# Routing steps of a fused attention and expert kernel held in PSUM

## The chip, the cores and the metric

The kernel runs on one core of a Trainium2 chip. The core has five engines with a queue each: PE (TensorE) multiplies matrices and transposes, DVE (VectorE) and ACT (ScalarE) do element-wise work and reductions, POOL (GpSimd) adds and subtracts in SBUF here and issues indirect DMAs, SP (SyncE) issues the other DMAs. [...] The metric is the device time of one execution in microseconds (us); before the change three runs took 1650.76, 1652.64 and 1657.65 us.

## The reference

Three layers follow each other. The first is attention with keys and values pooled by 8, over 8 batches, 8 heads, 576 rows of 64 values (4608 tokens of 512). The second sends each token to the one of 8 experts with the largest logit. The third is a gated layer with 1536 hidden values.

```python
k_p = k.reshape(B, H, Sp, pool, D).mean(axis=3)
v_p = v.reshape(B, H, Sp, pool, D).mean(axis=3)
scores = scale * np.matmul(q, k_p.transpose(0, 1, 3, 2))
attn = softmax(scores)                      # max subtracted
x = np.matmul(attn, v_p)                    # 4608 tokens x 512

logits = x @ w_gate
expert_idx = np.argmax(logits, axis=1)
for e in range(E):
    mask = expert_idx == e
    h = np.maximum(x[mask] @ w1[e], 0.0)
    out[mask] = gate_w[mask, None] * (h @ w2[e])

xn = x / rms * rms_g
g = xn @ w_gate2
out = (g * sigmoid(g) * (xn @ w_val)) @ w_out
```

## The kernel before

**The attention loop.** `for n in range(NTL)` (L809) goes over 36 tiles of 128 tokens. A tile's body is written out in a fixed order: transposes of its probabilities (emit_pt, L417), the exponentials of the tile after it (emit_exp), the turned queries three tiles ahead (emit_qt), place a, the scores two tiles ahead (emit_sc, PSUM tile sc), place b, the product with the values (emit_av, PSUM tile av; DVE then divides, L450 to L462, and writes the logits of the tile into lgs), the store of the tile before, and the places c, d and e. Each engine runs its own instructions in the order in which they were written.

**The places.** Everything else is put into the places a to e of a tile by `plan(n, where, f)`: loads and sums of keys and values (POOL adds groups of rows, L269 to L295, DVE some of them, L291), their transposes and scalings (rows_v, prep_vg, prep_k, place_v), the routing, the choice of the first expert, and the loads and splits of its weights. The table ORDER says at which place the steps on keys and values stand.

**Shared PSUM.** The pool `ps` has two buffers of one bank each, with the tags "pp" and "pq". A new tile of a tag waits until everybody has read the one before. "pq" holds turned queries; "pp" holds the turned sums of keys and values (ptk, ptv, pk), the values times the gate (pvg), half of the placed values (pv), ranks (rk), counts (cn0, cn) and half of a slot's turned rows (px).

**Routing.** Groups of four or five tiles are routed together (route_steps, L481). r1 finds each token's expert on DVE: the maximum of the logits (rmx), an equality (roh), a number for each candidate (rcd), its minimum (rcm), and the one-hot row rob. It stands in place d of the tile behind the group: tiles 4, 9, 13, 18, 22, 27, 31, 34, and inside the last tile. r3, two tiles later in place d, ranks the tokens: PE counts into rk, and nine DVE steps follow (L512 to L530), which mask, add, turn the rank into an address by bit operations, and bring the running counts run_c forward. r4 scatters the token numbers with indirect DMAs from POOL's queue.

**The first slot.** From tile 21 on the kernel chooses the expert with the most tokens (choose to choose_5), gathers its first 256 rows (first_rows, L655; tile xg), copies their logits to lg0 with POOL (L661), and turns the rows (xpose, L580) in tiles 32 and 33. The weights of this expert are loaded from tile 25 on (load_w) and split into a rounded part and a rest (split_w, L170): ACT casts (L148), POOL subtracts (L149), in 16 halves of 128x512. The first product with them stands in tile 34.

**Behind the loop** come 26 slots of 256 tokens for the experts and then the third layer; both are PE's matmuls almost throughout and are not touched.

Of the kernel before, what the change touches and what calls it, by code (L numbers as in the profile page):

```python
# [9 lines left out]
F32 = mybir.dt.float32  # L10
F32R = mybir.dt.float32r
BF16 = mybir.dt.bfloat16
I32 = mybir.dt.int32
U32 = mybir.dt.uint32
AF = mybir.ActivationFunctionType
ALU = mybir.AluOpType
AX = mybir.AxisListType
# [5 lines left out]
DM = 512  # L23
E = 8
F1 = 1024
F2 = 1536
T = 256
# [6 lines left out]
XW = DM + E  # L34
CUT = 18
# [16 lines left out]

R3 = [13, 17]

CW = [19, 30, 36, 46, 35, 52]

PLAIN = (0, 1, 2, 3, 4, 5)

# [24 lines left out]
def fused(ctx: ExitStack, tc: tile.TileContext, q, k, v, moe_w_gate, moe_w1, moe_w2,  # L83
          w_gate, w_val, w_out, rms_g, cst, out):
    nc = tc.nc
# [37 lines left out]
    lg0 = const.tile([128, 2, E], F32, name="lg0")  # L123
# [6 lines left out]
    def apart(i, key):  # L130

        i = getattr(i, "ins", i)
        nc.gpsimd.memset(spare, 0.0)
        for o in groups_.setdefault(key, []):
            tc.declare_no_dep(i, o, reason="rows of their own")
        groups_[key].append(i)
# [7 lines left out]
    def wtile(dt, name):  # L144
        return wp.tile([128, 1024], dt, tag="w", name=name)

    def split(hi, lo, src, eng=nc.vector):
        nc.scalar.copy(out=hi, in_=src)  # L148
        eng.tensor_tensor(out=lo, in0=src, in1=hi, op=ALU.subtract)  # L149
# [21 lines left out]
    def split_w(i, half, fresh=False):  # L171
        if fresh:
            for w, nm in ((w1h, "w1h"), (w1l, "w1l")) if i < 4 else ((w2h, "w2h"), (w2l, "w2l")):
                w[i % 4] = wtile(F32R, f"{nm}{i % 4}")
        hi, lo = (w1h[i], w1l[i]) if i < 4 else (w2h[i - 4], w2l[i - 4])
        c = slice(512 * half, 512 * half + 512)
        split(hi[:, c], lo[:, c], st[i][:, c], nc.gpsimd)
# [3 lines left out]
    sm_p = rctx.enter_context(tc.tile_pool(name="sm", bufs=2))  # L181
    sm1 = rctx.enter_context(tc.tile_pool(name="sm1", bufs=1))
    ps = rctx.enter_context(tc.tile_pool(name="ps_a", bufs=1, space=PSUM))
# [297 lines left out]
    def route_steps(n0, n1):  # L481
        n = n1 - n0
        t = {}

        def r1():
            lg = lgs[:, n0:n1]
            mx = sm_p.tile([128, n, 1], F32, tag="rmx", name="rmx")
            nc.vector.tensor_reduce(out=mx, in_=lg, axis=AX.X, op=ALU.max)
            mb = mx.to_broadcast([128, n, E])
            oh = sm1.tile([128, n, E], F32, tag="roh", name="roh")  # L490
            nc.vector.tensor_tensor(out=oh, in0=lg, in1=mb, op=ALU.is_equal)
            ie = cc[:, C_IE:C_IE + E].unsqueeze(1).to_broadcast([128, n, E])
            cand = sm1.tile([128, n, E], F32, tag="rcd", name="rcd")
            nc.vector.scalar_tensor_tensor(out=cand, in0=oh, scalar=-16.0, in1=ie, op0=ALU.mult, op1=ALU.add)
            cm = sm1.tile([128, n, 1], F32, tag="rcm", name="rcm")
            nc.vector.tensor_reduce(out=cm, in_=cand, axis=AX.X, op=ALU.min)
            ob = sm_p.tile([128, n, E], BF16, tag="rob", name="rob")
            nc.vector.tensor_tensor(out=ob, in0=cand, in1=cm.to_broadcast([128, n, E]), op=ALU.is_equal)
            t["ob"] = ob

        def r3():

            ob = t["ob"]
            rk = ps.tile([128, n, E], F32, tag="pp", name="rk")
            nc.tensor.matmul(rk, lhsT=tri, rhs=ob, start=True, stop=False)
            nc.tensor.matmul(rk, lhsT=ones, rhs=off_c.unsqueeze(1).to_broadcast([128, n, E]), start=False, stop=False)
            for j in range(n - 1):
                nc.tensor.matmul(rk[:, j + 1:], lhsT=ones, rhs=ob[:, j:j + 1].to_broadcast([128, n - 1 - j, E]),
                                 start=False, stop=False)
            nc.tensor.matmul(rk, lhsT=ones, rhs=run_c.unsqueeze(1).to_broadcast([128, n, E]), start=False, stop=True)  # L510
            pos = sm_p.tile([128, n, E], F32, tag="rpo", name="rpo")
            nc.vector.tensor_tensor(out=pos, in0=rk, in1=ob, op=ALU.mult)  # L512
            pf = sm_p.tile([128, n], F32, tag="rpf", name="rpf")
            nc.vector.tensor_reduce(out=pf, in_=pos, axis=AX.X, op=ALU.add)
            pi = sm_p.tile([128, n], I32, tag="rpi", bufs=4, name="rpi")
            nc.vector.tensor_copy(out=pi, in_=pf)
            q_ = pf.bitcast(I32)
            nc.vector.tensor_scalar(out=q_, in0=pi, scalar1=15, scalar2=4,
                                    op0=ALU.bitwise_and, op1=ALU.logical_shift_left)
            nc.vector.scalar_tensor_tensor(out=q_, in0=pi, scalar=-T, in1=q_,  # L520
                                           op0=ALU.bitwise_and, op1=ALU.bitwise_or)
            nc.vector.tensor_scalar(out=pi, in0=pi, scalar1=4, scalar2=15,
                                    op0=ALU.logical_shift_right, op1=ALU.bitwise_and)
            nc.vector.tensor_tensor(out=pi, in0=q_, in1=pi, op=ALU.bitwise_or)
            if n == 1:
                nc.vector.tensor_tensor(out=run_c, in0=run_c, in1=ob[:, 0], op=ALU.add)
            else:
                more = sm_p.tile([128, E], F32, tag="rmo", name="rmo")
                nc.vector.tensor_reduce(out=more, in_=ob.rearrange("p n e -> p e n"), axis=AX.X, op=ALU.add)
                nc.vector.tensor_tensor(out=run_c, in0=run_c, in1=more, op=ALU.add)  # L530
            t["pi"] = pi
            if n1 == CUT:
                nc.vector.tensor_copy(out=run_1, in_=run_c)

        def r4(j):
            def f():
                i = nc.gpsimd.indirect_dma_start(
                    out=ord_d[:, :], out_offset=bass.IndirectOffsetOnAxis(ap=t["pi"][:, j:j + 1], axis=0),
                    in_=tok[:, n0 + j:n0 + j + 1], in_offset=None)
                apart(i, "ord")  # L540
            return f

        return r1, r3, [r4(j) for j in range(n)]

    xts, hs, p1 = {}, {}, []
# [34 lines left out]
    def xpose(s, c):  # L580

        px_ = px(c)
        for d in range(2):
            for z in range(2):
                nc.tensor.transpose(px_[:, d, 128 * z:128 * z + 128],
                                    xg[s][:, z, (2 * c + d) * 128:(2 * c + d) * 128 + 128], ident)
        hi, lo = (x[:, 2 * c:2 * c + 2] for x in xts[s])
        nc.scalar.copy(out=hi, in_=px_)
        nc.vector.tensor_tensor(out=lo, in0=px_, in1=hi, op=ALU.subtract)
        if c and s:  # L590
            gate_of(s)


    ev, xg, first = {}, {}, {}
# [60 lines left out]
    def first_rows():  # L655
        xg[0] = x_p.tile([128, 2, XW], F32, tag="xg0", bufs=1, name="xg0")
        for z in range(2):
            nc.gpsimd.indirect_dma_start(
                out=xg[0][:, z], out_offset=None, in_=x_d[0:CUT * 128, :],
                in_offset=bass.IndirectOffsetOnAxis(ap=tok0[:, z:z + 1], axis=0))  # L660
        nc.gpsimd.tensor_copy(out=lg0, in_=xg[0][:, :, DM:XW])  # L661
        xts[0] = tuple(wtile(F32R, "xt0").rearrange("p (c t) -> p c t", c=4) for _ in range(2))

    def second_tokens():
# [10 lines left out]
    def px(c):  # L675
        return ps.tile([128, 2, T], F32, tag=("pq", "pp")[c], name="px")
# [4 lines left out]
    def plan(n, where, f):  # L681
        at.setdefault((n, where), []).append(f)
# [13 lines left out]
    for name, soon, later in ORDER:  # L696
        for m in range(1, 4):
            i = soon if m == 1 else later
# [10 lines left out]
    for n0, n1 in groups:  # L709
# [9 lines left out]
        for j, f in enumerate(r4):  # L719
            plan(n1 + R3[1] // 5 + j // 2, "abcde"[R3[1] % 5], f)  # L720
    for i, f in zip(CW, (choose, first_expert, first_tokens, first_rows)):
        plan(CUT + i // 5, "abcde"[i % 5], f)
    for i in range(8):
        plan(CUT + 7 + i // 2, "ac"[i % 2], lambda i=i: load_w(i, ev[0], True))
        plan(CUT + 9 + (i + 1) // 2, "ca"[i % 2], lambda i=i: split_w(i, 0, True))
        plan(CUT + 9 + (i + 1) // 2, "eb"[i % 2], lambda i=i: split_w(i, 1))
    plan(CUT + 4, "e", choose_2)
    plan(CUT + 7, "e", choose_3)
    plan(CUT + 8, "e", choose_4)
    plan(CUT + 9, "e", choose_5)  # L730
    plan(SECOND - 2, "a", second_tokens)
    plan(SECOND, "c", second_rows)
    plan(NTL - 4, "b", lambda: xpose(0, 1))
    plan(NTL - 3, "a", lambda: xpose(0, 0))
    plan(NTL - 3, "b", start_slots)

# [445 lines left out]
    for s in range(SURE):  # L1182
# [15 lines left out]
        a = unit_steps(s, 0)  # L1198
# [206 lines left out]
```

## Time and profile before

| what | value |
|---|---|
| three runs | 1650.76, 1652.64, 1657.65 us |
| the profiled execution's own time | 1641.33 us |
| its span in the profile | 1639.5 us |
| PE busy | 1590.8 us, 97% of the span |
| DVE busy | 850.8 us, 52% |
| ACT busy | 500.8 us, 31% |
| POOL busy | 263.5 us, 16% |
| attention loop | about the first 228 us |

The profile shows one execution. Its span is the time from the first to the last instruction that the hardware profiler recorded; the execution's own time is 1.83 us longer. "Busy" is the time in which an engine worked on an instruction; the rest is idle. A row of the timeline gives the start, the length, the engine, the line of the kernel, the operation, what it writes and reads, and how many instructions were merged; in brackets stand the idle time of the engine before it and what ended that.

### The profile page before, as it was taken

The page shows a single profiled execution, that of the slowest core. Times are in us where ns is not written, and L with a number is a line of the kernel's source. Part 1 is how long each engine was busy: PE and PEld are TensorE (multiplying, and loading weights), DVE is VectorE, ACT ScalarE, POOL GpSimd, SP SyncE. Part 2 cuts the span into 40 slices and gives each one's busy share as a digit, 9 for nine tenths or more (in the row PEclk, how much of TensorE's full clock was granted, in tenths as well). Part 3 has the DMA queues.
Part 4 walks back from the last instruction along what each step waited for, and adds up shares of the span by engine and source line. Part 5 has one row for each costly group of instructions (what it writes and reads, how often), then busy time and mean ns, then how long its engine had stood idle before and what let it go on. Part 6 is the DMA issues. An engine that isn't in the chain of part 4 may idle for free. (4 is left out here: it accounts for less than half of the span.)

```text
span 1639.5 us, 26570 instructions
## 1 busy us (share of the span) xinstructions
PE 1590.8 (97%) x9331; PEld 1373.4 (84%) x9332; DVE 850.8 (52%) x1824; ACT 500.8 (31%) x1052; POOL 263.5 (16%) x362
## 2 busy tenths in 40 slices
PE   9999899999999989999999999999999999999997
PEld 6888889977888888889788888888888888888886
DVE  7688876788758687225433433334343333443222
ACT  3454633545434453222212122121211212122121
POOL 5776552110111101103000000000000000000000
PEclk9999999999999999999999999999999999999999
DMA  7965636476746464219201000010010001000000
GB/s 216 287 190 152 178 94 214 139 264 229 245 147 216 156 219 123 67 35 322 59 13 33 20 14 26 14 39 13 20 33 14 26 13 39 14 1 26 1 26 14
DMA packets 125373, 161.97 MB, mean 99 GB/s; under 512 B 38544, under 2 KB 83728, under 8 KB 125216
## 3 DMA queue, kind: packets, MB, share of 16 engines
q1 hardware_dynamic: 113440, 124.13, 25.5%
q0 software_dynamic: 11776, 35.91, 7.0%
q8 instruction: 78, 1.28, 0.3%
q14 instruction: 79, 0.65, 0.1%
HBM read 116.92 MB, written 43.08 MB: 98 GB/s over the span
## 5 line engine op out<-in xcount | busy, mean ns | idle before, releaser
L1302 DVE SCALAR_TENSOR_TENSOR th<-th,g 128x512 f32<-128x512 f32 (+1 forms) x120 | 76.1, 634 | 469.0 <-ACT th L1301 469.0
L1299 PE MATMUL g<-xh,rl 128*128 128x512 f32 (+1 forms) x576 | 217.3, 377 | 0.0
L1298 PE MATMUL g<-xl,rh 128*128 128x512 f32 (+1 forms) x576 | 217.3, 377 | 0.0
L1297 PE MATMUL g<-xh,rh 128*128 128x512 f32 (+1 forms) x576 | 217.2, 377 | 0.0
L1301 ACT ACTIVATE th<-g 128x512 f32<-128x512 f32 (+1 forms) x120 | 66.8, 557 | 461.9 <-PE g L1299 461.9
L1328 POOL DMA_INDIRECT out_dram<-o,tk x36 | 34.6, 962 | 815.7 <-ACT o L1327 786.4
L1323 PE MATMUL po<-rl,a 128*128 128x512 f32 x360 | 140.3, 390 | 1.5 <-DMA rl<-scr 1.5
L1322 PE MATMUL po<-rh,a 128*128 128x512 f32 x360 | 140.2, 389 | 0.0
L1324 PE MATMUL po<-rh,a 128*128 128x512 f32 x360 | 140.1, 389 | 0.0
L1298 PEld LDWEIGHTS g<-xl,rh 128*128 128x128 f32 x576 | 108.3, 188 | 20.3
L1297 PEld LDWEIGHTS g<-xh,rh 128*128 128x128 f32 x576 | 108.3, 188 | 20.3
L1299 PEld LDWEIGHTS g<-xh,rl 128*128 128x128 f32 x576 | 108.4, 188 | 20.0
L148 ACT CAST a<-th 128x512 fp32r<-128x512 f32 (+1 forms) x120 | 69.3, 578 | 167.2 <-DVE th L1303 167.2
L554 PE MATMUL p<-xh,w1h 128*128 128x256 f32 x672 | 109.3, 285 | 10.8 <-DVE hl L557 8.3
L149 DVE TENSOR_TENSOR a<-th,a 128x512 fp32r<-128x512 f32 (+1 forms) x120 | 76.7, 639 | 77.3 <-ACT a L148 77.3
L1297 PE MATMUL g<-xh,uh 128*128 128x512 f32 (+1 forms) x288 | 108.7, 378 | 1.7 <-DVE th L1303 1.7
L1298 PE MATMUL g<-xl,uh 128*128 128x512 f32 (+1 forms) x288 | 108.6, 377 | 0.0
L1299 PE MATMUL g<-xh,ul 128*128 128x512 f32 (+1 forms) x288 | 108.6, 377 | 0.0
L554 PE MATMUL p<-xh,w1l 128*128 128x256 f32 x672 | 107.3, 282 | 0.0
L554 PE MATMUL p<-xl,w1h 128*128 128x256 f32 x672 | 106.8, 281 | 0.0
L554 PEld LDWEIGHTS p<-xh,w1h 128*128 128x128 f32 x672 | 93.2, 191 | 15.9 <-DVE hl L557 9.4
L557 DVE SCALAR_TENSOR_TENSOR hl<-p,hh 128x256 fp32r<-128x256 f32 x168 | 70.6, 421 | 62.0 <-ACT hh L556 54.4
(289 smaller groups left out, 3019.2 us busy)
## 6 DMA issues: line engine op xcount, KB each, us to landing
st<-in_moe_w_dram SPq DMA_DIRECT2D x64, 512.0 KB
y_d<-ys SPq DMA_DIRECT2D x39, 257.0 KB
v<-in_v_dram SPq DMA_DIRECT2D x32, 288.0 KB
y<-y_d SPq DMA_DIRECT2D x68, 128.0 KB
x_d<-x SPq DMA_DIRECT2D x32, 260.0 KB
q<-in_q_dram SPq DMA_DIRECT2D x15, 512.0 KB
scr<-uh SPq DMA_DIRECT2D x13, 512.0 KB
scr<-ul SPq DMA_DIRECT2D x13, 512.0 KB
```

The costliest lines, as they stand in the source:

```text
L148: nc.scalar.copy(out=hi, in_=src)
L149: eng.tensor_tensor(out=lo, in0=src, in1=hi, op=ALU.subtract)
L554: nc.tensor.matmul(a, lhsT=w[d][:, fs], rhs=x[:, d], start=j + d == 0, stop=j == 2 and d == 3)
L557: nc.vector.scalar_tensor_tensor(out=lo, in0=a, scalar=0.0, in1=hi, op0=ALU.max, op1=ALU.subtract)
L1297: nc.tensor.matmul(g[:, j], lhsT=wh[:, sl], rhs=hi[:, d], start=d == 0, stop=False)
L1298: nc.tensor.matmul(g[:, j], lhsT=wh[:, sl], rhs=lo[:, d], start=False, stop=False)
L1299: nc.tensor.matmul(g[:, j], lhsT=wl[:, sl], rhs=hi[:, d], start=False, stop=d == 3)
L1301: nc.scalar.activation(out=th, in_=g[:, 0], func=AF.Tanh, scale=0.5)
L1302: nc.vector.scalar_tensor_tensor(out=th, in0=th, scalar=1.0, in1=g[:, 0], op0=ALU.add, op1=ALU.mult)
L1322: nc.tensor.matmul(po, lhsT=a[:, 0, tsl], rhs=wh[:, sl], start=c == 0, stop=False)
L1323: nc.tensor.matmul(po, lhsT=a[:, 0, tsl], rhs=wl[:, sl], start=False, stop=False)
L1324: nc.tensor.matmul(po, lhsT=a[:, 1, tsl], rhs=wh[:, sl], start=False, stop=c == NC2 - 1)
```

## The change

r1 allocates a PSUM tile rw of tag "pp", copies the logits into it, and holds the equality and the candidates there. r3 holds the sum, the address and the counts' increment in the unused part of rk's bank. The logits lg0 are copied by ACT in xpose, directly behind the transposes, where POOL copied them behind the gather. The splits of the weights get their places from a table SPLIT, both halves of one in the same place. choose_2 goes from place e of tile 22 to d of tile 23, choose_5 from e of tile 27 to a of tile 28. The shortened list CW drops a number that nothing read.

```diff
-CW = [19, 30, 36, 46, 35, 52]
+CW = [19, 30, 36, 46, 35]
+
+SPLIT = [(27, "a"), (27, "c"), (28, "a"), (28, "c"), (30, "c"), (31, "a"), (32, "a"), (32, "c")]
...
-            oh = sm1.tile([128, n, E], F32, tag="roh", name="roh")
-            nc.vector.tensor_tensor(out=oh, in0=lg, in1=mb, op=ALU.is_equal)
+            w = ps.tile([128, 3, n, E], F32, tag="pp", name="rw")
+            nc.vector.tensor_copy(out=w[:, 0], in_=lg)
+            nc.vector.tensor_tensor(out=w[:, 1], in0=w[:, 0], in1=mb, op=ALU.is_equal)
...
-            cand = sm1.tile([128, n, E], F32, tag="rcd", name="rcd")
-            nc.vector.scalar_tensor_tensor(out=cand, in0=oh, scalar=-16.0, in1=ie, op0=ALU.mult, op1=ALU.add)
+            nc.vector.scalar_tensor_tensor(out=w[:, 2], in0=w[:, 1], scalar=-16.0, in1=ie, op0=ALU.mult, op1=ALU.add)
...
-            nc.vector.tensor_tensor(out=ob, in0=cand, in1=cm.to_broadcast([128, n, E]), op=ALU.is_equal)
+            nc.vector.tensor_tensor(out=ob, in0=w[:, 2], in1=cm.to_broadcast([128, n, E]), op=ALU.is_equal)
...
-            rk = ps.tile([128, n, E], F32, tag="pp", name="rk")
+            rt = ps.tile([128, 64], F32, tag="pp", name="rk")
+            rk = rt[:, 0:n * E].rearrange("p (n e) -> p n e", e=E)
...
-            pf = sm_p.tile([128, n], F32, tag="rpf", name="rpf")
+            pf = rt[:, 48:48 + n]
             nc.vector.tensor_reduce(out=pf, in_=pos, axis=AX.X, op=ALU.add)
+            pw = rt[:, 56:56 + n].bitcast(I32)
+            nc.vector.tensor_copy(out=pw, in_=pf)
+            q_ = sm_p.tile([128, n], I32, tag="rpf", name="rpf")
+            nc.vector.tensor_scalar(out=q_, in0=pw, scalar1=15, scalar2=4,
+                                    op0=ALU.bitwise_and, op1=ALU.logical_shift_left)
...
-                more = sm_p.tile([128, E], F32, tag="rmo", name="rmo")
+                more = rt[:, 40:40 + E]
...
+        if c and not s:
+            nc.scalar.copy(out=lg0, in_=xg[0][:, :, DM:XW])
...
-        nc.gpsimd.tensor_copy(out=lg0, in_=xg[0][:, :, DM:XW])
...
-        plan(CUT + 9 + (i + 1) // 2, "ca"[i % 2], lambda i=i: split_w(i, 0, True))
-        plan(CUT + 9 + (i + 1) // 2, "eb"[i % 2], lambda i=i: split_w(i, 1))
-    plan(CUT + 4, "e", choose_2)
+        n, w = SPLIT[i]
+        plan(n, w, lambda i=i: split_w(i, 0, True))
+        plan(n, w, lambda i=i: split_w(i, 1))
+    plan(CUT + 5, "d", choose_2)
...
-    plan(CUT + 9, "e", choose_5)
+    plan(CUT + 10, "a", choose_5)
```

Where it tells in the order of the instructions. On PE, tile 27 before: the product with the values (av), then in place e the values times the gate (pvg), then the next tile's transposes (pt). In brackets stands on which engines' signals a row waits.

```order
L443 MATMUL av<-vbd_131,ptsb 128x146 [waits Activation_49]
L443 MATMUL av<-vbd_131,ptsb 128x146 x2
L349 MATMUL pvg<-wg,vt 72x16 [waits Activation_49]
L349 MATMUL pvg<-wg,vt 72x16 x3
L425 MATMUL pt<-cc,pe 96x128 x6
```

The same place on PE in the changed kernel:

```order
L445 MATMUL av<-vbd_131,ptsb 128x146 [waits Activation_49]
L445 MATMUL av<-vbd_131,ptsb 128x146 x2
L351 MATMUL pvg<-wg,vt 72x16 [waits DVE_49,Activation_49]
L351 MATMUL pvg<-wg,vt 72x16 x3
L427 MATMUL pt<-cc,pe 96x128 x6
```

The rows stand where they stood; the first pvg now waits for DVE as well, for its instruction that writes rob in the same tile. On DVE the same tile before: the end of the division (x), r1, choose_5 (quant), second_tokens (tokc), the maximum of the next scores (mx).

```order
L462 TENSOR_TENSOR x<-av,rs 128x512 [waits DMAHW6_49]
L488 TENSOR_REDUCE rmx<-lgs 128x5
L491 TENSOR_TENSOR roh<-lgs,rmx 128x40 [waits DVE_49]
L494 SCALAR_TENSOR_TENSOR rcd<-roh,cc 128x40 [waits DVE_49]
L496 TENSOR_REDUCE rcm<-rcd 128x5 [waits DVE_49]
L498 TENSOR_TENSOR rob<-rcd,rcm 128x40 [waits DVE_49]
L638 TENSOR_SCALAR m_2499<-cc 128x8
L639 SCALAR_TENSOR_TENSOR quant<-m_2499 128x8 [waits DVE_49]
L640 TENSOR_SCALAR quant<-lam 128x8
L641 MEMSET quant 128x8
L665 TENSOR_SCALAR tokc<-tok_88 128x2 [waits DMASW5_49,DMASW4_49]
L408 TENSOR_REDUCE mx<-sc 128x8 [waits PE_49]
```

And on DVE in the changed kernel:

```order
L464 TENSOR_TENSOR x<-av,rs 128x512 [waits DMAHW6_49]
L490 TENSOR_REDUCE rmx<-lgs 128x5
L493 COPY rw<-lgs 128x40 [waits Activation_49]
L494 TENSOR_TENSOR rw<-rw,rmx 128x40 [waits DVE_49]
L496 SCALAR_TENSOR_TENSOR rw<-rw,cc 128x40 [waits DVE_49]
L498 TENSOR_REDUCE rcm<-rw 128x5 [waits DVE_49]
L500 TENSOR_TENSOR rob<-rw,rcm 128x40 [waits DVE_49]
L644 TENSOR_SCALAR m_2530<-cc 128x8
L645 SCALAR_TENSOR_TENSOR quant<-m_2530 128x8 [waits DVE_49]
L646 TENSOR_SCALAR quant<-lam 128x8
L647 MEMSET quant 128x8
L670 TENSOR_SCALAR tokc<-tok_88 128x2 [waits DMASW5_49,DMASW4_49]
```

The copy has come in, and waits until ACT has read what was in the buffer; choose_5 keeps its neighbours. On POOL, from the gather (xg) of tile 27 on, before: the copy of the logits (lg) stands behind the gather, and all subtractions (w1l) behind the copy.

```order
L658 DMA xg_2451<-x_d,tok_88 128x520 [waits DMAHW4_49,DMAHW3_49,DMAHW2_49]
L658 DMA xg_2451<-x_d,tok_88 128x520
L661 COPY lg_91<-xg_2451 128x16 [waits DMASW3_49,DMASW2_49]
L149 TENSOR_TENSOR w1l_2476<-st_2285,w1h_2475 128x512 [waits DMAHW1_49,Activation_49]
L149 TENSOR_TENSOR w1l_2476<-st_2285,w1h_2475 128x512 [waits Activation_49]
L149 TENSOR_TENSOR w1l_2528<-st_2330,w1h_2527 128x512 [waits DMAHW4_49,Activation_49]
```

The same stretch of POOL in the changed kernel:

```order
L151 TENSOR_TENSOR w1l_2425<-st_2280,w1h_2424 128x512 [waits DMAHW1_49,Activation_49]
L151 TENSOR_TENSOR w1l_2425<-st_2280,w1h_2424 128x512 [waits Activation_49]
L664 DMA xg_2452<-x_d,tok_88 128x520 [waits DMAHW4_49,DMAHW3_49,DMAHW2_49]
L664 DMA xg_2452<-x_d,tok_88 128x520
L151 TENSOR_TENSOR w1l_2476<-st_2325,w1h_2475 128x512 [waits DMAHW4_49,Activation_49]
```

The first two subtractions now stand ahead of the gather, the copy is gone, and nothing on POOL waits for the gather's landing.

## Rows read from the trace of the kernel before

**Rows 1.** The page, part 1: busy us, share of the span, instructions.

```profile
PE 1590.8 (97%) x9331; PEld 1373.4 (84%) x9332; DVE 850.8 (52%) x1824; ACT 500.8 (31%) x1052; POOL 263.5 (16%) x362
```

**Rows 2.** Stretches: us; PE, PEld, DVE, ACT, POOL busy; PE clock, DMA, GB/s.

```profile
160.00:170.00 10.00, 9.53 (x83) 8.85 (x83) 7.71 (x26) 3.28 (x8) 5.56 (x7) 0.83 0.52 164
200.00:210.00 10.00, 8.63 (x52) 8.62 (x52) 7.09 (x21) 4.88 (x11) 9.15 (x11) 0.68 0.09 28
340.00:350.00 10.00, 7.92 (x54) 7.72 (x53) 9.01 (x18) 5.83 (x12) 0.54 (x1) 0.83 0.87 294
390.00:400.00 10.00, 8.33 (x63) 7.68 (x63) 9.12 (x14) 8.14 (x15) 0.84 (x2) 1.00 0.89 324
```

**Rows 3.** Waits of PE, 0 to 260 us: total us, times, longest.

```profile
PE sc L401 <- DVE rs L450: 4.7, 1, 4.7
PE sc L404 <- DVE rs L450: 2.9, 2, 2.1
...
PE pv L361 <- ACT qt L391: 0.7, 1, 0.7
PE av L443 <- DVE x L462: 0.5, 2, 0.3
```

**Rows 4.** Timeline, tiles 30 to 32: start, us, engine, instruction, idle before.

```profile
189.79 9.87 POOL L149 TENSOR_TENSOR w1l<-st,w1h 128x512 fp32r<-128x512 f32 x8
...
192.41 1.15 DVE L516 CAST rpi<-rpf 128x5 int32<-128x5 f32 x1
...
198.63 1.05 DVE L530 TENSOR_TENSOR run_c<-run_c,rmo 128x8 bf16<-128x8 bf16 x1
...
201.37 2.26 PE L401 MATMUL sc<-kbd,qt 128*128 128x144 f32 x8 [4.73 <-DVE rs L450]
```

**Rows 5.** Timeline, tile 22, a step of r1.

```profile
155.04 1.49 DVE L498 TENSOR_TENSOR rob<-rcd,rcm 128x32 bf16<-128x32 f32 x1
```

**Rows 6.** Timeline, tile 27: PE's pvg and DVE's r1.

```profile
179.51 0.64 PE L349 MATMUL pvg<-wg,vt 128*72 128x16 f32 x8
...
181.19 0.18 DVE L488 TENSOR_REDUCE rmx<-lgs 128x5 f32<-128x40 f32 x1
181.41 0.20 DVE L491 TENSOR_TENSOR roh<-lgs,rmx 128x40 f32<-128x40 f32 x1
...
182.11 0.20 DVE L498 TENSOR_TENSOR rob<-rcd,rcm 128x40 bf16<-128x40 f32 x1
```

**Rows 7.** Timeline, tiles 4 and 13: r1's start and PE's place e.

```profile
48.74 0.18 DVE L488 TENSOR_REDUCE rmx<-lgs 128x4 f32<-128x32 f32 x1
48.94 1.59 PE L327 MATMUL pk<-cc,se 96*128 96x48 f32 x8 [0.83 <-ACT kbd L331]
...
103.34 1.65 PE L361 MATMUL pv<-vau,both 72*96 72x146 f32 x12
...
105.05 0.17 DVE L488 TENSOR_REDUCE rmx<-lgs 128x4 f32<-128x32 f32 x1
```

**Rows 8.** Timeline, tile 7: r3's first step, POOL, and pvg.

```profile
65.01 0.45 POOL L295 TENSOR_TENSOR sv<-v 72x128 f32<-72x128 f32 x1 [3.41 <-ACT vau L315]
65.18 0.18 DVE L512 TENSOR_TENSOR rpo<-rk,rob 128x32 f32<-128x32 f32 x1
...
66.35 0.69 PE L349 MATMUL pvg<-wg,vt 128*72 128x16 f32 x8
```

**Rows 9.** Timeline, tiles 32 and 35: r1 and PE's next use of pp.

```profile
208.05 0.18 DVE L488 TENSOR_REDUCE rmx<-lgs 128x4 f32<-128x32 f32 x1
...
208.44 0.60 PE L585 MATMUL px<-cc,xg 128*128 128x128 f32 x4
...
223.65 0.19 PE L505 MATMUL rk<-rob,tri 128*128 128x32 bf16 x1
...
224.03 0.17 DVE L498 TENSOR_TENSOR rob<-rcd,rcm 128x8 bf16<-128x8 f32 x1
```

**Rows 10.** Timeline: POOL's copy of the first slot's logits.

```profile
189.63 0.19 POOL L661 COPY lg<-xg 128x16 f32<-128x16 f32 x1 [11.63 <-DMA xg<-x_d,tok]
```

More of the change, by code (lines that the diff above doesn't have):

```diff
@@ L489, in r1 @@
             mb = mx.to_broadcast([128, n, E])
-            oh = sm1.tile([128, n, E], F32, tag="roh", name="roh")
-            nc.vector.tensor_tensor(out=oh, in0=lg, in1=mb, op=ALU.is_equal)
+            w = ps.tile([128, 3, n, E], F32, tag="pp", name="rw")
+            nc.vector.tensor_copy(out=w[:, 0], in_=lg)
+            nc.vector.tensor_tensor(out=w[:, 1], in0=w[:, 0], in1=mb, op=ALU.is_equal)
             ie = cc[:, C_IE:C_IE + E].unsqueeze(1).to_broadcast([128, n, E])
-            cand = sm1.tile([128, n, E], F32, tag="rcd", name="rcd")
-            nc.vector.scalar_tensor_tensor(out=cand, in0=oh, scalar=-16.0, in1=ie, op0=ALU.mult, op1=ALU.add)
+            nc.vector.scalar_tensor_tensor(out=w[:, 2], in0=w[:, 1], scalar=-16.0, in1=ie, op0=ALU.mult, op1=ALU.add)
             cm = sm1.tile([128, n, 1], F32, tag="rcm", name="rcm")
-            nc.vector.tensor_reduce(out=cm, in_=cand, axis=AX.X, op=ALU.min)
+            nc.vector.tensor_reduce(out=cm, in_=w[:, 2], axis=AX.X, op=ALU.min)
             ob = sm_p.tile([128, n, E], BF16, tag="rob", name="rob")
-            nc.vector.tensor_tensor(out=ob, in0=cand, in1=cm.to_broadcast([128, n, E]), op=ALU.is_equal)
+            nc.vector.tensor_tensor(out=ob, in0=w[:, 2], in1=cm.to_broadcast([128, n, E]), op=ALU.is_equal)
             t["ob"] = ob
@@ L512, in r3 @@
             nc.vector.tensor_tensor(out=pos, in0=rk, in1=ob, op=ALU.mult)
-            pf = sm_p.tile([128, n], F32, tag="rpf", name="rpf")
+            pf = rt[:, 48:48 + n]
             nc.vector.tensor_reduce(out=pf, in_=pos, axis=AX.X, op=ALU.add)
-            pi = sm_p.tile([128, n], I32, tag="rpi", bufs=4, name="rpi")
[L516 to L524, printed above, removed]
+            pw = rt[:, 56:56 + n].bitcast(I32)
[3 more added lines that the diff above has]
+                                    op0=ALU.bitwise_and, op1=ALU.logical_shift_left)
+            nc.vector.scalar_tensor_tensor(out=q_, in0=pw, scalar=-T, in1=q_,
+                                           op0=ALU.bitwise_and, op1=ALU.bitwise_or)
+            nc.vector.tensor_scalar(out=pw, in0=pw, scalar1=4, scalar2=15,
+                                    op0=ALU.logical_shift_right, op1=ALU.bitwise_and)
+            pi = sm_p.tile([128, n], I32, tag="rpi", bufs=4, name="rpi")
+            nc.vector.tensor_tensor(out=pi, in0=pw, in1=q_, op=ALU.bitwise_or)
             if n == 1:
```

## The prediction

> **What bounds the kernel now.** I read the page first: PE is busy for 97% of the span, DVE for half of it [rows 1]. The change touches only the first 230 us, the attention loop of 36 tiles, so the question is what PE does there. PE's waits over the first 260 us come next: the reader is to see how little there is to win, and that the largest items are PE waiting for DVE [rows 3]. Scores wait for their PSUM tile until DVE has finished the tile before: 4.7 and 2.9 us; with 0.7 (a copy by ACT behind a late DVE) and 0.5 that makes 8.8 us. The rest of the stretch PE has no idle time worth naming, so whatever is put in PE's way there costs its full length. [...]
>
> Why DVE is late is seen in the timeline. While POOL subtracts weight halves back to back, DVE's routing steps r3 on 128x5 values take 1.15 and 1.05 us [rows 4]; in tile 22 a step of r1 takes 1.49 [rows 5]. The same kind of step takes 0.20 us when POOL is quiet [rows 6]. So the steps stand still while a POOL operation runs, and PE's 4.73 us stop at 201.37 follows from six such steps.
>
> **What the change takes away.** With one operand in PSUM the steps should no longer stand still: the multiply that reads rk from PSUM took 0.18 us although POOL was in the middle of an addition of 0.45 us [rows 8]. The r3 ahead of that stop then ends some 6 us earlier, in tiles 22 to 24 DVE gains 2 us or more, and the 8.8 us of PE idle time go. The clock loses less too: 0.17 of 10 us = 1.7 us after the smaller stop; 0.32 of 10 = 3.2 us after the larger, of which 0.7 fell into the stop itself (it ended at 201.37): 2.5. Together 4.2 us. What is late next there is nothing but PE's own matmuls. So the gain is 8.8 + 4.2 = 13.0 us.
>
> **What the change adds.** One copy per group: nine, 0.2 us each, on an engine that is not the bound. But r1 now takes the one buffer of tag "pp", which PE needs for the turned keys and values. r1 stands in place d of a tile; in tiles 4, 9, 13, 18, 22 and 27 a step in place e writes "pp" next, and the instruction order shows that PE's first matmul there now waits for DVE as well. DVE must first divide that tile's output (it starts when av ends), then do r1's six steps. Behind the waiting matmul stands the whole next tile in PE's queue.
>
> The price comes from the rows of before. Steps of r1 follow each other every 0.23 us: four of them from 181.19 to 182.11 [rows 6]. With one more, rob ends 5 x 0.23 + 0.20 = 1.35 us after rmx begins. Tile 27: rmx at 181.19, so rob ends at 182.54, but pvg went to PE at 179.51 [rows 6]: 3.03 us. Tile 13: 105.05 + 1.35 - 103.34 = 3.06. Tiles 9, 18 and 22 have the same shape, 3.03 to 3.06 each. Tile 4: 48.74 + 1.35 - 48.94 = 1.15, since PE waits there for ACT anyway [rows 7]. Sum of the six: 16.4 us.
>
> Three smaller ones. r3 now holds "pp" until its ninth step: 65.18 + 8 x 0.23 + 0.2 = 67.2, and pvg of tile 7 started at 66.35 [rows 8]: 0.85. The turned rows of the first slot: 208.05 + 1.35 - 208.44 = 0.96. The last group's rk starts at 223.65 and must now wait for the last r1, which with one step more ends at 224.40: 0.76 [rows 9]. Added idle time of PE: 16.4 + 2.6 = 19.0 us.
>
> **The clock after the new stops.** Of four 10 us stretches in which PE stood still for about 2 us or more, three show a clock of 0.83 or less, one shows 1.00 [rows 2]. The loss was 1.7 us for a stop of 2 us. Five new stops of 3 us: 5 x 3/4 x 1.7 = 6.4 us, between 0 (none) and 8.5 (all).
>
> Sum: 19.0 - 8.8 - 4.2 + 6.4 = +12.4 us. On the profiled execution's own 1641.33 us that is 1653.7. The median of the runs shown, 1652.64, lies 11.3 us above that execution; nothing in the change acts on the difference, so I add the same 12.4 us to the median: 1665.
>
> **What the trace of before does not show.** No DVE instruction there copies from SBUF into PSUM. The nearest rows bound it: 0.17 to 0.20 us like a free step, or held like the cast at 192.41 with 1.15 us [rows 4]. I take 0.2, as reads from PSUM run free; held in the four places where POOL adds values at that moment, it would add 4 x 1.0 = 4 us to the stops. [...]
>
> Does a step in PSUM take longer by itself? A multiply out of PSUM on 128x32 took 0.18 us [rows 8], one with both operands in SBUF on 128x40 0.20 [rows 6]: no surcharge. [...]
>
> **Parts at nothing.** lg0: POOL waited 11.63 us for the gather before it copied the logits [rows 10]; now ACT copies them in tile 32, some 0.2 us, long after the gather has landed. POOL starts the subtractions earlier, but PE wants the first split weights in tile 34 only, so no PE time comes from that. SPLIT moves the same 16 ACT casts and 16 POOL subtractions; the two gathers now stand behind the first two subtractions, two additions of 1.3 us and a wait later, and they landed at 189.63 [rows 10] for transposes at 208.44 [rows 9]: 19 us of cover. POOL gets fuller in tiles 30 to 33; the rank scatters stand behind it, and were they to come late at the end of the loop, 1 to 3 us would be added, which the upper end holds. choice's step 2 stands one tile later on DVE; SP reads its result early in tile 24, with one store of x queued behind: under 1 us. Step 5 keeps its neighbours on DVE.
>
> **Rivals.** [...]
> (2) Faster. PE's matmul in place e doesn't hold up anything, because the time is made good: if DVE is ahead and r1 follows av at once, only the gains remain, -13.0: 1639.6. Its place is tile 13; it decides if PE goes from av to pv in under 0.5 us. Against it: DVE had been waiting for av's end in the rows, so it can't be earlier.
> (3) The change doesn't do what it says: steps with PSUM operands stand still as well. Then the 13.0 us stay, and each stop grows by the held steps, up to 1 us each, some 2.5 us in four places: 19.0 + 8.5 + 10 = +37, 1690. Against: rk's multiply beside POOL's addition [rows 8].
>
> **How the numbers follow.** Forecast 0.64, rival 1 0.20, rival 2 0.08, rival 3 0.08. A difference under 0.5%, 8.3 us, can't be told from none. The forecast's own range is 1658.6 to 1671 (copies held, all clocks down: +18.5); some 0.07 of its 0.64 fall within 0.5%. So slower 0.57 + 0.08 = 0.65, same 0.27, faster 0.08. Run to run the three times spread over 7 us; for 8 in 10 I take 1653 to 1674.
>
> **What would show it.** Right: in the profile after, PE's waits list pvg and pv behind DVE rob with about 3 us in tiles 9, 13, 18, 22 and 27; the r3 steps take 0.2 us beside POOL's subtractions; the scores' 4.7 us are gone; clock values of 0.83 stand after the new stops. Wrong: PE's idle time in the first 240 us falls, or the steps in PSUM still take 1 us or more.

## The result, and the profile after

The changed kernel takes 1669.31 us (median of five runs, 1668.2 to 1672.41), the kernel before 1656.4 us in the five runs beside and ahead of it (1650.76 to 1657.65). The ratio is 1.0091, 95% interval 1.007 to 1.0112: slower, by 12.9 us between these medians. In four later groups the kernel before had medians of 1653.86 to 1655.3 us (29, 18, 23 and 10 runs); against those the loss is 14 to 15.5 us.

The page of the changed kernel, part 1; its columns are those of [rows 1]:

```profile
PE 1599.0 (96%) x9331; PEld 1381.3 (83%) x9332; DVE 835.7 (50%) x1833; ACT 501.3 (30%) x1053; POOL 262.9 (16%) x361
```

DVE has nine instructions more than in [rows 1] and is busy for 15 us less: fewer of the small steps stand still (r3's cast and its last addition take 0.16 to 0.17 us each time, where [rows 4] had 1.15 and 1.05; choice's first step still stands, for 3.09 us in tile 27). PE is busy for 8 us more with the same matmuls: part of them ran at a lower clock, and the mean that was granted over the span is 0.984, before 0.991. PE's waits in the first 270 us of the changed kernel, against [rows 3]:

```profile
PE pv L363 <- DVE rob L500: 7.0, 2, 3.8
PE pvg L351 <- DVE rcm L498: 4.6, 1, 4.6
PE ptv L303 <- DVE rob L500: 3.1, 1, 3.1
PE pvg L351 <- DVE rob L500: 2.9, 1, 2.9
PE rk L508 <- DVE rob L500: 2.8, 1, 2.8
PE pk L329 <- DVE rob L500: 2.1, 1, 2.1
...
PE px L589 <- DVE rob L500: 0.7, 1, 0.7
...
PE pvg L351 <- DVE run_c L534: 0.7, 1, 0.7
```

The scores' waits for rs are gone. In their place PE waits nine times, 23.8 us in all, and all but the last row name r1's steps. One of these stops, tile 9, in the timeline of the changed kernel:

```profile
84.99 0.68 DVE L464 TENSOR_TENSOR x<-av,rs 128x512 f32<-128x512 f32 x1
85.31 0.72 POOL L272 TENSOR_TENSOR sk<-k 128x256 f32<-128x256 f32 x1
85.59 0.19 DVE L490 TENSOR_REDUCE rmx<-lgs 128x5 f32<-128x40 f32 x1
85.69 0.19 DVE L493 COPY rw<-lgs 128x40 f32<-128x40 f32 x1
...
86.64 0.20 DVE L500 TENSOR_TENSOR rob<-rw,rcm 128x40 bf16<-128x40 f32 x1
86.98 0.71 PE L303 MATMUL ptv<-cc,sv 72*128 72x72 f32 x4 [3.09 <-DVE rob L500]
87.49 1.49 PE L427 MATMUL pt<-cc,pe 128*96 128x128 f32 x6
```

The six steps take 1.25 us from rmx to rob's end; the copy takes 0.19 us in the middle of an addition of POOL. PE stood still for 3.09 us, and then six transposes took 1.49 us where they take 0.82 elsewhere. In tile 13 the product pv, 1.65 us in [rows 7], took almost twice as long:

```profile
115.59 3.21 PE L363 MATMUL pv<-vau,both 72*96 72x146 f32 x12 [3.81 <-DVE rob L500]
118.59 1.49 PE L427 MATMUL pt<-cc,pe 128*96 128x128 f32 x6
```

The stretches of the changed kernel that hold these stops (columns as in [rows 2]):

```profile
80.00:90.00 10.00, 6.91 (x58) 6.03 (x58) 5.91 (x15) 4.70 (x11) 8.80 (x12) 0.83 0.27 53
90.00:100.00 10.00, 10.00 (x85) 9.29 (x82) 5.10 (x9) 3.81 (x10) 4.03 (x6) 0.83 0.43 130
110.00:120.00 10.00, 6.19 (x34) 5.91 (x33) 3.85 (x13) 2.30 (x6) 9.37 (x14) 0.69 0.07 27
140.00:150.00 10.00, 7.09 (x54) 6.17 (x53) 4.00 (x13) 3.24 (x9) 6.88 (x9) 0.73 0.47 92
```

The clock fell behind all seven stops of 2 us or more (the stretches not shown read 0.71, 0.83, 0.80 and 0.83), and behind tile 9's it was still low in the next stretch, in which PE was never idle. Behind the two stops of 0.7 us it stayed at 1.00.

Profile against profile the difference is larger than between the medians: spans of 1639.5 and 1666.4 us. The profiled execution of before was a favourable one, as the first experiment shows.

### The profile page after: what moved, and what is told of

It reads as the page before. It is cut to its first block, busy times and chain, and to the rows that moved or that the text cites. A ratio compares the mean times of both kernels' runs of the same rounds, so it can differ in the third digit from the quotient of the medians.

```text
span 1666.4 us, 26579 instructions
## 1 busy us (share of the span) xinstructions
PE 1599.0 (96%) x9331; PEld 1381.3 (83%) x9332; DVE 835.7 (50%) x1833; ACT 501.3 (30%) x1053; POOL 262.9 (16%) x361
## 5 line engine op out<-in xcount | busy, mean ns | idle before, releaser
L1305 PEld LDWEIGHTS g<-xh,rl 128*128 128x128 f32 x576 | 108.3, 188 | 19.9
L558 PEld LDWEIGHTS p<-xh,w1h 128*128 128x128 f32 x672 | 91.7, 189 | 18.9 <-DVE hl L561 11.1
```

The source lines that it names most:

```text
L558: nc.tensor.matmul(a, lhsT=w[d][:, fs], rhs=x[:, d], start=j + d == 0, stop=j == 2 and d == 3)
L1305: nc.tensor.matmul(g[:, j], lhsT=wl[:, sl], rhs=hi[:, d], start=False, stop=d == 3)
```

## The experiments

Theory 1: r1's tile rw stands ahead of place e's step in the one buffer of pp, and PE pays with the stops and with the clock behind them. Theory 2: r3's longer hold on pp does it. Theory 3: the moved splits, copy and steps of choice do it. All ratios are to runs of the kernel before on the same chip; brackets hold 95% intervals.

**Before, unchanged.**

```diff
(no line differs)
```

> The kernel before, unchanged, for a second profile and its spread. Theory A (the level of the profiled execution is chance): the ratio is 1.000 within 0.002, and the second profile has an own time nearer to the median of 1656 than the first one's 1641, with more idle time or a lower granted clock at places that can be named, 8 to 15 us of it. Theory B (a profiled execution of this kernel is always some 11 us shorter than an unprofiled one, while the changed kernel's is not): the second profile again stands near 1641.

Measured: 1654.09 us, 1.0011 [1.0, 1.0022]; the profiled execution took 1652.44 us. Theory A. Against the first profile this one had lost 4.5 us by tile 35, 7.3 by the third set of turned rows (248 us) and 8.7 by the first row of the third layer. The first 28 matmuls of that layer cost another 2.3 us, as the clock was low there in this execution (0.77 over 750 to 760 us, against 1.00 in the first profile's 740 to 750 us). The first and the last of the 28, in the first profile and then in the second:

```profile
740.62 0.38 PE L1297 MATMUL g<-y0t,uh 128*128 128x256 f32 x1 [3.48 <-ACTq L1218]
...
743.95 0.28 PE L1297 MATMUL g<-y0t,uh 128*128 128x256 f32 x1
```

```profile
749.28 0.58 PE L1297 MATMUL g<-y0t,uh 128*128 128x256 f32 x1 [3.69 <-ACTq L1218]
...
754.96 0.29 PE L1297 MATMUL g<-y0t,uh 128*128 128x256 f32 x1
```

From there to the end every row stands 11.0 to 11.1 us later. The scores' 4.7 us behind rs [rows 3] were 1.9 this time:

```profile
PE sc L404 <- DVE rs L450: 2.7, 2, 2.1
PE sc L401 <- DVE rs L450: 1.9, 1, 1.9
PE av L443 <- DVE x L462: 1.7, 4, 0.9
```

How long DVE's steps stand still beside POOL, and which of them, differs from execution to execution: here r1 of tile 27 was caught as well (three of its steps took 0.78, 1.19 and 0.96 us), and three steps of r3, at 1.19 to 1.20 us, instead of six.

**r1 alone, r3 alone, the rest alone.**

```diff
 r1 alone: r1 as in the changed kernel
+            w = ps.tile([128, 3, n, E], F32, tag="pp", name="rw")
...
 r3 alone: r3 as in the changed kernel
+            rt = ps.tile([128, 64], F32, tag="pp", name="rk")
...
 rest alone: lg0 by ACT, SPLIT, choose_2 and choose_5 as in the changed kernel
+        plan(n, w, lambda i=i: split_w(i, 0, True))
...
```

> Only r1 takes the PSUM tile of tag pp; r3, the logits of the first slot, the splits and choice's steps are as before. Theory 1 (the loss is r1's tile standing ahead of place e's use of pp): PE waits of 2 to 4 us for rob in tiles 4, 9, 13, 18, 22 and 27, some 20 us in all, as in the changed kernel, and the scores' 4.7 and 2.9 us behind rs stay, since r3 still stands still beside POOL. Slower than before by 20 to 30 us (the loss of 12.9 and the 8 to 13 that r3 no longer gives back). Theory 2 (r3's longer hold on pp is the loss): no change within 4 us. Theory 3 (the moved splits and copies are the loss): no change within 4 us.

> Only r3 holds its values in rk's PSUM bank; all else as before. Theory 1: faster by 8 to 13 us: the scores' 4.7 us behind rs go, most of the 2.9 too, one stop of some 0.8 us (pvg behind run_c, tile 7) comes. Theory 2: slower by 8 us or more, with stops behind run_c in several tiles. Theory 3: faster by under 5 us or the same.

> r1 and r3 as before; the copy of the first slot's logits by ACT, the table of splits and the two moved steps of choice as in the changed kernel. Theories 1 and 2: the same within 4 us; the scores' waits behind r3 change place but not size, as POOL subtracts as much as before. Theory 3: slower by 8 us or more, with PE waits behind choice's steps, the splits or tile 27's stretch that before did not have.

Measured: r1 alone 1674.87 us, 1.0132 [1.0117, 1.0146], +21.0; r3 alone 1649.53, 0.9974 [0.9962, 0.9986], -4.3; the rest alone 1647.72, 0.9964 [0.9951, 0.9976], -6.1. With r1 alone the stops behind rob are those of the changed kernel (6.9, 2.9, 2.9, 2.1 us and so on); of the scores' waits, expected to stay, 2.9 us are left. So the loss is r1's; theories 2 and 3 fall, since both other parts gain.

But r3 alone gains less than expected, and the rest gains where nothing was expected. With r3 alone its steps do run free, beside the same subtractions that held them in [rows 4]:

```profile
199.46 4.98 POOL L149 TENSOR_TENSOR w2l<-st,w2h 128x512 fp32r<-128x512 f32 x4
199.65 0.17 DVE L517 CAST rk<-rk 128x5 int32<-128x5 f32 x1
```

The scores' 4.7 us are gone. In this one profile, however, PE stands for 4.46 us ahead of the last tile's product with the values, behind DVE, which was itself idle for 4.11 us until something that the profile doesn't name; the clock falls to 0.67 in 220 to 230 us. Whether other executions have this stop isn't known.

What the rest gains is seen in the timeline of the kernel with the rest alone. Its r3 is in SBUF, as before, and yet:

```profile
195.33 0.17 DVE L518 CAST rpi<-rpf 128x5 int32<-128x5 f32 x1
195.53 0.17 DVE L520 TENSOR_SCALAR rpf<-rpi 128x5 int32<-128x5 int32 x1
...
196.59 1.00 POOL L539 DMA_INDIRECT ord_d<-tok,rpi  x1 [3.02 <-DVE rmo L531]
```

The table SPLIT leaves a gap between POOL's subtractions, and r3 falls into it: 0.17 us a step where [rows 4] had 1.15, with POOL idle. r3 in PSUM and the moved splits remove the same wait, the scores' 4.7 us behind rs, each alone. That the 6.1 us come from the splits, and not from lg0 or choice, is read from this and was not tried apart.

**r1 in place e, in SBUF, in the other bank.**

```diff
 place e
-        plan(n1, "d", r1)
+        plan(n1, "e", r1)
...
 SBUF: the changed kernel with r1 of before
-            w = ps.tile([128, 3, n, E], F32, tag="pp", name="rw")
...
 other bank
-            w = ps.tile([128, 3, n, E], F32, tag="pp", name="rw")
+            w = ps.tile([128, 3, n, E], F32, tag="pq", name="rw")
```

> The changed kernel with r1 in place e of its tile, behind that place's step on keys and values, instead of place d ahead of it; the r1 inside the last tile stays. Theory 1 (order in pp is the loss): the stops of 2 to 4.6 us in tiles 4, 9, 13, 18, 22 and 27 go, and most of the clock falls behind them; what is left of the stops is under 6 us, most of it rk's 2.8 in the last tile. DVE's copy into rw now waits for the reader of place e's tile, so the next tile's first DVE step may come up to 1 us later each time. 15 to 27 us faster than the changed kernel, that is 1643 to 1656, 0.990 to 1.000 of before. Theory 2 or 3: no change against the changed kernel within 4 us.

> The changed kernel with r1 as before, in SBUF; r3, the copy of the logits, the splits and choice's moves stay changed. Theory 1: no stop behind rob is left, some 20 us of PE's idle time and most of the clock falls go; the fastest so far: 8 to 13 us faster than before, 1643 to 1648 (0.992 to 0.995). Theory 2: as slow as the changed kernel within 4 us, with stops behind run_c. Theory 3: as slow as the changed kernel less a few us.

> The changed kernel with r1's tile in the other shared bank, tag pq, which PE needs next for the turned queries of the next tile, behind the transposes of probabilities. Theory 1 (a stop is as long as DVE's end of rob lies behind the moment PE would take the bank): PE has 1.5 to 2.5 us more work before it comes to pq than to pp, so each stop shrinks from 3 us to 0.5 to 1.5, and stops stand in all of r1's tiles, the two without a step in place e too; sum of the stops 4 to 10 us; 1648 to 1660. If the clock falls after any stop, whatever its length, the time stays near the changed kernel's, 1663 or more; if only after long ones, it comes near 1650.

Measured: place e 1640.41 us, 0.9917 [0.9891, 0.9943], the fastest; SBUF 1648.38, 0.9963 [0.9949, 0.9977]; the other bank 1655.86, 1.0013 [0.9999, 1.0027]. The same six steps, with the same tile in the same bank, behind PE's step instead of ahead of it: 28.9 us (25.5 in a later group of runs, below). Theory 1 holds. SBUF is 5.5 us faster than before, less than the 8 to 13 expected. PE's waits in the first 270 us with place e:

```profile
PE rk L508 <- DVE rob L500: 2.6, 1, 2.6
PE pvg L351 <- ACT vt L316: 2.4, 1, 2.4
PE sc L403 <- DVE pe L412: 1.6, 1, 1.6
```

The stops behind rob are gone but for the last tile's and one of 0.7 us. The 2.4 us stand in tile 27 and are place e's own: DVE and ACT were idle there as well, released by something that the profile doesn't name, and the clock fell (0.81 in 170 to 180 us).

In bank pq stops of 12.0 us in all remain under rob's name, more than the 4 to 10 expected: that bank is also written by half of pv (4.9 us) and by the first slot's product (3.8 us), which I had left out. Two more, of 2.04 and 2.18 us, are put down to ACT, but pq starts 0.11 us after rob's end there: 16.2 us in all. Not each of them brought the clock down: behind the 2.21 us of tile 22 it stayed at 1.00.

r1 in PSUM at place e also does what it was made for. In the same kernel, tile 27, r1's last steps and choose_5's first:

```profile
180.44 7.40 POOL L151 TENSOR_TENSOR w1l<-st,w1h 128x512 fp32r<-128x512 f32 x6
180.65 0.20 DVE L500 TENSOR_TENSOR rob<-rw,rcm 128x40 bf16<-128x40 f32 x1
180.76 7.12 DVE L644 TENSOR_SCALAR m<-cc 128x8 f32<-128x8 f32 x1
...
187.91 0.17 DVE L645 SCALAR_TENSOR_TENSOR quant<-m 128x8 f32<-128x8 f32 x1
```

While POOL runs six subtractions in a row, rob, which reads PSUM, takes 0.20 us; the next step, from SBUF to SBUF on a fifth of the values, stands for 7.12 us until POOL is done.

**Three stops.** Place e for all but tiles 9, 13 and 18.

```diff
-        plan(n1, "e", r1)
+        plan(n1, "d" if n1 in (9, 13, 18) else "e", r1)
```

> The kernel with r1 in place e, but the r1 of tiles 9, 13 and 18 back in place d, as in the changed kernel: three of the six stops alone (3.1, 3.8 and 2.9 us, 9.8 in all). It asks what a stop costs in all. A stop costs its own length and the clock holds: 9.8 us slower than with all in place e, 1650. The forecast's size, 1.3 us of clock per stop: 1654. The size that the starts of the tiles show in the changed kernel, some 2.8 us of clock per stop (6.1, 6.1 and 5.9 us of delay across these tiles): 18 us slower, 1658.

Measured: 1659.7 us, 1.0032 [1.0018, 1.0046]: 19.3 us slower than with none (15.9 against a later group of runs of that kernel, below), for 9.8 us of standing still. That is the third size, 5.3 to 6.4 us a stop. The twelve runs spread over 12.5 us.

**The stops filled.** The changed kernel, with PE kept at work in them.

```diff
+    def fill(k):
+        def f():
+            z = pa.tile([128, 4, 128], F32, tag="p0", name="fl")
+            for _ in range(k):
+                nc.tensor.matmul(z, lhsT=ones,
+                                 rhs=ones.unsqueeze(1).to_broadcast([128, 4, 128]), start=True, stop=True)
+        return f
...
+        if n1 in (4, 9, 13, 18, 22, 27):
+            plan(n1, "d", fill(5 if n1 == 4 else 10))
```

> The changed kernel with matmuls of no use (ones by ones, 512 columns, result read by nobody) on PE between av and place e's step in tiles 4 (five of them), 9, 13, 18, 22 and 27 (ten each, some 2.3 us at full clock). DVE's end of rob stays where it is, so PE comes to pp at the same moment as in the changed kernel; only its idle time is filled. If the clock falls because PE stands still: the granted clock stays at 1.00 behind these six places, and the kernel is 12 to 17 us faster than the changed one, 1652 to 1657. If the clock falls for another reason, or doesn't matter: the same as the changed kernel, 1667 to 1671. If the filling itself is in the way: slower than that.

Measured: 1654.69 us, 0.9999 [0.9986, 1.0013], 14.6 us faster than the changed kernel, with 55 matmuls more (9386 for 9331 in the pages). Its tile 9, and the stretch:

```profile
88.81 0.47 PE L303 MATMUL ptv<-cc,sv 72*128 72x72 f32 x4 [1.06 <-DVE rob L500]
89.11 0.82 PE L427 MATMUL pt<-cc,pe 128*96 128x128 f32 x6
```

```profile
90.00:100.00 10.00, 10.00 (x100) 9.45 (x100) 6.13 (x10) 5.74 (x15) 5.27 (x7) 1.00 0.57 147
110.00:120.00 10.00, 8.36 (x49) 6.83 (x48) 3.93 (x14) 4.18 (x12) 9.37 (x13) 0.83 0.07 27
```

PE still comes to pp only when rob is done, but the transposes behind it take 0.82 us, not 1.49. Of the six places only tile 13, where filling left 1.64 us of idle time, shows a fall. (One more, 0.83 in 30 to 40 us, stands ahead of all six, behind a wait of 2.36 us for loaded queries.) So it is PE's standing still that brings the clock down here: filled, it read 1.00 behind five of the six stops, where the changed kernel has 0.71 to 0.83. The stops last as long as before, only filled; keeping PE at work in them is worth the 14.6 us.

The starts of the transposes of tiles 9 and 11 give the same per stop, first without it (place e), then in the changed kernel, then with three stops, then with filling:

```profile
77.09 0.82 PE L427 MATMUL pt<-cc,pe 128*96 128x128 f32 x6
...
88.22 0.82 PE L427 MATMUL pt<-cc,pe 128*96 128x128 f32 x6
```

```profile
79.37 0.82 PE L427 MATMUL pt<-cc,pe 128*96 128x128 f32 x6
...
96.66 0.82 PE L427 MATMUL pt<-cc,pe 128*96 128x128 f32 x6
```

```profile
76.04 0.82 PE L427 MATMUL pt<-cc,pe 128*96 128x128 f32 x6
...
93.10 0.82 PE L427 MATMUL pt<-cc,pe 128*96 128x128 f32 x6
```

```profile
81.07 0.82 PE L427 MATMUL pt<-cc,pe 128*96 128x128 f32 x6
...
95.53 0.82 PE L427 MATMUL pt<-cc,pe 128*96 128x128 f32 x6
```

11.13 us; 17.29, or 6.16 more; 17.06, or 5.93 more; 14.46, or 3.33 more (1.06 us idle, 2.32 us of filling). Of the 6.16, 3.09 is the stop and 3.07 the clock. The same subtraction between changed kernel and place e, over the two tiles from each stop on:

| stop in tile | delay, us | idle time added | clock |
|---|---|---|---|
| 4 | 4.02 | 2.07 - 0.83 | 2.8 |
| 9 | 6.16 | 3.09 | 3.1 |
| 13 | 6.09 | 3.81 | 2.3 |
| 18 | 5.86 | 2.91 | 2.95 |
| 22 | 4.85 | 3.15 | 1.7 |

Tile 27 is left out, since place e has a stop and a fall of its own there. Tile 4's fall needs no long stop: behind the 0.83 us that before has there, the clock fell in the first profile of before (0.86 in 50 to 60 us) and stayed at 1.00 in the second.

**Without the rest; the last r1 in SBUF; place e again.**

```diff
 without the rest: place e and r3 in PSUM, lg0, splits and choice as before
 last r1 in SBUF: place e, and
-            w = ps.tile([128, 3, n, E], F32, tag="pp", name="rw")
+            if n > 1:
+                w = ps.tile([128, 3, n, E], F32, tag="pp", name="rw")
+            else:
+                w = sm1.tile([128, 3, n, E], F32, tag="roh", name="rw")
 place e again: no line differs
```

> r1 (in place e) and r3 with their values in PSUM, but the copy of the first slot's logits on POOL, the splits and the two steps of choice as before. Alone, those other parts were worth 6 us, and r3 alone 4. If each part takes its own waits away: 6 us slower than with all parts, 1646 to 1647. If the parts take the same wait away (the scores behind steps that stand still beside POOL's subtractions), so that with r1 and r3 in PSUM the other parts are worth nothing more: 1639 to 1642.

> The kernel with r1 in place e (1640.4 us, 0.992 of before), and in addition the r1 of the last tile, which handles one group row, in SBUF again. In the last tile PE then has no need to wait for rob before it counts into rk: the 2.6 us stop there shrinks to the 1.3 us that before had, behind run_c. Theory 1: 1 to 3 us faster than with that r1 in PSUM, 1636 to 1641, the fastest of all. Theory 2 or 3: no opinion beyond no change; 1638 to 1643.

> The kernel with r1 in place e once more, unchanged: the same kernel with one more step in SBUF came out 5.6 us slower, against what was expected. If the earlier 1640.4 us stands, the ratio is again 0.989 to 0.994, and the last tile's r1 in SBUF has a price that has to be found. If it was a favourable group of runs, it comes out at 0.994 to 0.997 (1644 to 1648), and the two kernels can't be told apart.

Measured: without the rest 1645.01 us, 0.9938 [0.9923, 0.9953]; the last r1 in SBUF 1645.97, 0.9947 [0.9927, 0.9967]; place e again 1643.81, 0.9931 [0.9909, 0.9954]. The last r1 in SBUF was a miss: rk then waits 3.1 us for run_c instead of 2.6 for rob, so the wait has only changed its name. Place e is faster than before in both groups, by 13.5 and 11.5 us, but these three versions can't be told apart, and what the rest adds to place e (1 to 5 us) stays open.

## Why the prediction was right, and where its sizes were off

The forecast was 1665.0, +12.4; measured 1669.3, +12.9 beside the same runs and some +15 against the later, larger groups. The mechanism is the one forecast, r1's stops ahead of place e's step with the clock falling behind them. That the sum comes so close is in part luck: the clock's term was half of what it measured, and much of what was taken away came from elsewhere than I said. Step by step:

**The added stops: right in place and kind, a little small.** Foreseen 16.4 us in six tiles and 2.6 in three; measured 19.6 (18.8 without the 0.83 that tile 4 had before) and 4.2. Tiles 9, 18 and 22 have 3.09, 2.91 and 3.15 us for 3.03 to 3.06. Larger are tile 13 (3.81), where rmx came 2.47 us after av's end, as DVE was still subtracting the maximum from the next tile's scores, while in [rows 7] it came 1.71 us after pv's start; tile 27 (4.56), where DVE started the next scores' maximum late, for a reason that the profile doesn't show, and divided behind it; and rk in the last tile (2.76 for 0.76), where PE had nothing left to do before it. The copy ran free, in 0.16 to 0.19 us each time: the lower bound.

**The clock behind the stops: mis-sized.** Foreseen 1.3 us a stop, 6.4 in all, from a fall that cost 1.7 and three cases out of four. All five stops of the table brought the clock down, at 1.7 to 3.1 us each: 12.8 in all, and 14.6 by filling. (The forecast's five were tiles 9, 13, 18, 22 and 27; the four that both have cost 10.) The four cases were also misread: PE's idle time in the stretches of [rows 2] is 0.47, 1.37, 2.08 and 1.67 us, and the stops that brought the first two down begin in the stretch before. This is the term that failed. Rival 1, with a chance of 0.20, left it out: the clock holds at 1.00 behind the new stops, 19.0 - 8.8 - 4.2 = +6.0, which is the 1658.6 at the lower end of the range. The runs showed 0.69 to 0.83 behind the changed kernel's stops of 2 us or more, and a kernel 14.6 us faster with six of them filled.

**What was taken away: right in sum, wrong in its parts.** The changed kernel without r1's stops is place e: -13.5 and -11.5 us with its own small stops inside, where the prediction's terms give -13.0 + 2.6 = -10.4. But I gave all of it to the steps in PSUM and counted the rest at nothing. Alone the rest is worth 6.1 us, as the moved splits leave r3 a gap; r3 in PSUM is worth 4.3 alone and nothing beside them (both together 5.5). The failed step is "no PE time comes from that": I asked when PE wants the weights, not beside which steps of DVE the moved subtractions run. The further 5 to 8 us between r1 in SBUF and r1 in place e stand behind the loop for the most part (by its end the two profiles differ by 0.7 us, at the first row of the third layer by 3.5, a few us later by 4.6), and why they do isn't settled. So far as these 5 to 8 us go, the fit of -10.4 is luck.

**The level of the first profile.** I added the difference to the median and was right to: the second profile of before lies 11.1 us above the first. The terms 4.7 and 4.2 (the 4.2 from the clocks of 0.83 and 0.68 in [rows 2]), however, were read from that one execution, and another had 1.9 us in the place of the 4.7. Between this second profile and the changed kernel's, the delay is 19.9 us at the third set of turned rows, 16.7 at the first row of the third layer and 15.7 a few us later: 4 us come back in between, with two falls of the clock in place of three. Whether the later start causes that was not tried.

**The rivals.** Rival 2 (PE makes the time good) falls by the stops, rival 3 (steps in PSUM stand still as well) by rob's 0.20 us beside 7.40 us of POOL and by r3's cast, 0.17 us beside 4.98. No surcharge shows on a step that reads PSUM: r1's steps on 128x40 take 0.19 to 0.21 us in PSUM, 0.20 in SBUF [rows 6]. The copy into PSUM, for which the trace of before had no row, ran free, in 0.19 us beside POOL's addition of 0.72. Why steps in SBUF stand still beside POOL (1.15 us for the cast in [rows 4]) and those with a value in PSUM don't, no run here shows.

## What to carry to other kernels

A shared bank is a place in a queue: a tile that DVE fills over a microsecond belongs behind PE's next use of that bank, not ahead of it; the same work one place later was worth 25 to 29 us here. Three stops of 9.8 us in all cost this busy PE 16 to 19 us, for the clock behind them (5.93 us of delay at tile 9's stop of 3.1); where the stops were left in, useless matmuls in them paid, by 14.6 us. When two edits go for the same wait, don't add their gains; and read the size of such a wait from two profiles.

## What the runs showed of the hardware that was not expected

A step of 128x8 values on DVE, SBUF to SBUF, took 7.12 us beside six subtractions of POOL in a row (7.40 us), while the step ahead of it, which reads PSUM, took 0.20. In [rows 4] six steps of this kind took only 1.05 to 1.20 us each, beside eight subtractions in a row (9.87 us). What decides between the two isn't shown. And from some 5 us into the third layer to the end, nearly 900 us, the distance between the two profiled executions of the kernel before grows by no more than 0.07 us, though they were 11 us apart when they came to it: what sets these two apart arises in the loop, in the slots and in the first matmuls behind them.
